# Linear attention into a top-1 mixture of experts: table rows by a one-hot, loads of the second expert behind gathers, paired narrow tiles, new plan keys

## The chip, the cores and the metric

One core of a Trainium2 chip. The metric is device time in microseconds of one execution. The kernel before takes 562.57 us, the median of 3 runs (562.14 to 563.09).

## The reference

Attention without softmax, a norm per head, and a mixture of experts with one expert per token, 4608 tokens of 512, 8 experts.

```
kv  = einsum('bhsd,bhse->bhde', k, v)          # 8 batches, 8 heads, 576 tokens, 64
out = einsum('bhsd,bhde->bhse', q, kv)
x   = out / sqrt(mean(out*out, -1) + 1e-6) * g_norm     # as rows of 4608 x 512
expert = argmax(x @ w_gate); gate = softmax(x @ w_gate)[expert]
# each expert takes its tokens in order, up to capacity
y = relu(x[tokens of e] @ w1[e]) @ w2[e]       # 512 x 1024 and 1024 x 512
out[token] = gate[token] * y
```

## The kernel before

Attention runs by batch. Tokens' heads are multiplied by the small kv matrix, squares are summed, logits and gates follow, and the unnormed rows with their factors go to x_dram in device memory. Each batch also enters its tokens in a table: for each expert, 6 columns of 128 slots (W = 48 columns), which token stands where. Tokens reach their experts by an indirect DMA (a gather) from x_dram with row numbers from that table.

The expert that has most tokens after three batches is fixed as the first (`pick`, line 1077). Its weights are loaded during attention, and after the fifth batch its first 384 slots are gathered and multiplied (`early_slots`, line 1168). The others are ranked by their number of tokens when attention is over (`rank_experts`, line 1090), and each rank has a fixed budget of slots (line 19: 704, 672, 640, 624, 592, 576, 560, 512). The first expert's slots 384 to 704 are done next, then the seven others.

At the seam, `finish` (line 1302) reads the table (`read_table`), cuts the first expert's 6 columns out of it at an address held in a register (`slots`, line 647), makes the target rows (`targets`) and ranks the experts. `rows` (line 1189) gathers the first expert's rest in three tiles; `rows_beside` (line 1618) gathers each later expert's in up to six, norms them, splits them into a high and a low half (`pair`) and turns them by a DMA transpose on SP's queue. `weights` (line 1567) loads w1 and w2 of each later expert on SP's queue in four parts each, takes the largest absolute value on VectorE (tile am), scales, and splits them into high and low float16. SP reads the expert's number from perm_i.

The products of an expert are (high + low) x (high + low) without the last term, three float16 products. The first one (`Gemm1`, into hp) leaves hh and hl, the high and low halves of the hidden rows. The second one (`Gemm2`, into yp) has the hidden rows as the stationary operand in tiles of 128 rows. A last tile of at most 112 rows is done turned round (`turned_products`, line 592): weights stationary, the few rows moving, 24 matmuls for each of 4 blocks of outputs; the result is copied (`keep`), turned back and scaled. Narrow tiles here: 64, 32, 112, 80, 64 and 48 rows for experts 1, 2, 4, 5, 6 and 7 in order.

The order on all engines is fixed before the run by a planner (`Plan`, line 105). It has engines as servers with estimated durations, takes at each step the operation that can start soonest, and among those that can start together the one with the lowest key. WAIT allows an engine operations that start a little later than the soonest. There are two plans, one for attention and one for the experts. The keys of single operations are moved by a list of numbers (NUDGE, line 74; by the number of the operation). The real waits are semaphores put in by the framework from the data; an engine runs its list in order.

## Time and profile before

| | us |
|---|---|
| median of 3 runs | 562.57 |
| the profiled execution | 560.41 |
| its span, first to last instruction | 558.5 |

| engine | busy us | share of the span |
|---|---|---|
| TensorE (PE) | 518.9 | 93% |
| VectorE (DVE) | 395.4 | 71% |
| ScalarE (ACT) | 253.8 | 45% |
| GpSimd (POOL) | 156.1 | 28% |

PE is TensorE's matmuls and PEld its weight loads. SP issues DMAs only. In the lists, L598 is line 598 of the kernel; a tile's name stands left of the arrow where it is written, right where it is read. A bracket behind an instruction tells how long its engine sat idle before it and what ended that; "issue" is a wait with no cause in the profile. Attention reaches to about 155 us, the first expert's rest to about 200, the other experts to the end.

### The profile page before, as it was taken

The numbers are of one execution on the slowest core, as the hardware profiler recorded it, in microseconds if no ns is written. First come the engines' busy times: TensorE is split into PE (matmuls) and PEld (weight loads), VectorE is DVE, ScalarE is ACT, GpSimd is POOL, SyncE is SP. The second block draws the span as 40 slices with busy tenths as digits, with TensorE's granted clock in tenths as the row PEclk, the third lists the DMA queues.
The fourth block names the chain that finished last, engine by engine and source line by source line (L and its number), as shares of the span: only waits on it lengthen the run. The fifth ranks groups of instructions, "written<-read, shape, count | busy, mean of one in ns | idle before, by whom it ended". The sixth has DMA issues, their size and how long they took to land.

```text
span 558.5 us, 12272 instructions
## 1 busy us (share of the span) xinstructions
PE 518.9 (93%) x4727; PEld 343.5 (61%) x4727; DVE 395.4 (71%) x1033; ACT 253.8 (45%) x508; POOL 156.1 (28%) x175
## 2 busy tenths in 40 slices
PE   2989979798977989999999999999999999999994
PEld 2878778675535566546764575577467648745442
DVE  3388868999938789899899896796968537721200
ACT  0577747786414373283553643452553525211210
POOL 6011010662347363132305402350234041012011
PEclk9999979799999999999999999999999999999998
DMA  8999999854195769589475760972688070011010
GB/s 270 352 350 323 358 391 364 262 189 187 43 343 147 213 195 302 136 242 264 124 258 134 231 223 19 221 232 101 164 145 253 3 123 34 1 39 39 0 40 31
DMA packets 78021, 102.61 MB, mean 184 GB/s; under 512 B 43222, under 2 KB 51414, under 8 KB 76932
## 3 DMA queue, kind: packets, MB, share of 16 engines
q1 hardware_dynamic: 69600, 70.43, 43.0%
q0 software_dynamic: 7776, 31.30, 16.3%
q8 instruction: 39, 0.64, 0.5%
q14 instruction: 26, 0.21, 0.1%
q10 hardware_dynamic: 580, 0.02, 0.1%
HBM read 73.13 MB, written 20.61 MB: 168 GB/s over the span
## 4 chain that ended last, share of the span: by engine, by line
PE 50%; DMA 18%; issue 18%; DVE 7%; ACT 3%; POOL 2%; SPq 0%; POOLq 0%; DVEq 0%; ACTq 0%
PE hp L543 17%; PE yp L589 15%; DMA out_dram<-ysb,si 9%; PE op L843 5%; DMA xs<-pair 4%; PE a L754 3%; PE qp L825 2%; PE op L543 2%; DMA q_sb<-in_q_dram 2%; DMA v_sb<-in_v_dram 1%; DMA xg<-x_dram,gi 1%; PE yp L598 1%; PE op L589 1%; DVE ss L876 1%; POOL pair L488 1%
## 5 line engine op out<-in xcount | busy, mean ns | idle before, releaser
L543 PE MATMUL hp<-xs,w1h 128*128 128x320 f16 (+6 forms) x896 | 133.4, 300 | 4.3 <-DMA xs<-pair 1.6
L543 PEld LDWEIGHTS <-w1h 128*128 128x128 f16 x960 | 93.2, 98 | 43.6 <-issue 5.6
L619 POOL DMA_INDIRECT out_dram<-ysb,si x41 | 47.1, 1150 | 246.1 <-ACT ysb L614 133.0
L589 PEld LDWEIGHTS <-hh 128*128 128x128 f16 x560 | 54.4, 98 | 62.8 <-issue 0.4
L548 ACT ACTIVATE hh<-hp 128x320 f16<-128x320 f32 (+7 forms) x64 | 40.8, 638 | 105.7 <-PE hp L543 105.4
L354 DVE TENSOR_REDUCE am<-raw 128x1 f32<-128x512 f32 x120 | 76.3, 675 | 2.6 <-DMA raw<-in_moe_w_dram 2.6
L543 PE MATMUL hp<-xs,w1l 128*128 128x320 f16 (+6 forms) x448 | 71.5, 300 | 0.0
L551 DVE SCALAR_TENSOR_TENSOR hl<-hp,hh 128x320 f16<-128x320 f32 (+7 forms) x64 | 47.3, 739 | 33.4 <-ACT hh L548 32.8
L589 PE MATMUL yp<-w2h,hh 128*128 128x512 f16 x272 | 65.0, 379 | 0.2 <-ACT ysb L614 0.2
L589 PE MATMUL yp<-w2h,hl 128*128 128x512 f16 x272 | 65.1, 379 | 0.0
L589 PE MATMUL yp<-w2l,hh 128*128 128x512 f16 x272 | 64.7, 379 | 0.0
L614 ACT ACTIVATE ysb<-yp,ysc 128x512 f32<-128x512 f32 (+5 forms) x40 | 27.3, 682 | 81.1 <-PE yp L589 67.7
L543 PEld LDWEIGHTS <-w1l 128*128 128x128 f16 x480 | 46.8, 98 | 19.2
L450 POOL DMA_INDIRECT xg<-x_dram,gi x41 | 44.1, 1075 | 28.9 <-DVE xm L458 11.3
L589 PEld LDWEIGHTS <-hl 128*128 128x128 f16 x280 | 27.1, 98 | 31.8
L394 DVE SCALAR_TENSOR_TENSOR w1l<-raw,sg,w1h 128x512 f16<-128x512 f32 x64 | 45.1, 741 | 1.7 <-ACT w1h L388 1.7
L843 PE MATMUL op<-kv_bd,qt 128*128 128x144 f32 x256 | 43.9, 309 | 1.8 <-ACT qt L695 0.7
L394 DVE SCALAR_TENSOR_TENSOR w2l<-raw,sw,w2h 128x512 f16<-128x512 f32 x64 | 44.4, 742 | 0.3 <-ACT w2h L388 0.2
L388 ACT ACTIVATE w2h<-raw,sw 128x512 f16<-128x512 f32 x62 | 39.7, 711 | 6.2 <-PE yp L598 3.6
L843 PEld LDWEIGHTS op<-kv_bd,qt 128*128 128x128 f32 x256 | 36.4, 202 | 4.7 <-ACT qt L695 1.2
L388 ACT ACTIVATE w1h<-raw,sg 128x512 f16<-128x512 f32 x60 | 38.6, 711 | 1.6 <-DVE sg L383 1.6
L484 ACT CAST pair<-xm 128x512 f16<-128x512 f32 (+5 forms) x35 | 21.4, 616 | 39.3 <-DMA xs<-pair 20.3
(245 smaller groups left out, 685.2 us busy)
## 6 DMA issues: line engine op xcount, KB each, us to landing
raw<-in_moe_w_dram SPq DMA_DIRECT2D x64, 512.0 KB, 5.4
k_sb<-in_k_dram SPq DMA_DIRECT2D x16, 576.0 KB, 7.4
v_sb<-in_v_dram SPq DMA_DIRECT2D x16, 576.0 KB, 7.2
x_dram<-o_sb POOLq DMA_DIRECT2D x8, 1152.0 KB, 8.5
q_sb<-in_q_dram SPq DMA_DIRECT2D x16, 512.0 KB, 7.6
x_dram<-o_sb POOLq DMA_DIRECT2D x8, 144.0 KB, 8.5
q_sb<-in_q_dram SPq DMA_DIRECT2D x32, 32.0 KB, 6.8
xg<-x_dram,gi POOLq DMA_INDIRECT x41, 4.8
```

What stands on the lines that cost most here:

```text
L354: nc.vector.tensor_reduce(out=am()[:, p:p + 1], in_=raw[:, sl(p)], axis=AX.X, op=ALU.max, apply_absolute_value=True)
L388: nc.scalar.activation(wh[:, sl(p)], raw[:, sl(p)], AF.Copy, scale=z["s"])
L394: nc.vector.scalar_tensor_tensor(out=wl[:, sl(p)], in0=raw[:, sl(p)], scalar=z["s"], in1=wh[:, sl(p)], op0=ALU.mult, op1=ALU.subtract)
L450: nc.gpsimd.indirect_dma_start(out=self.xg[i][0:n], out_offset=None, in_=x_dram[0:self.rows, :], in_offset=bass.IndirectOffsetOnAxis(ap=se ...
L484: nc.scalar.copy(self.pair[i][0:n, 0], self.xm[i][0:n])
L543: nc.tensor.matmul(self.view(hp)[:, u], lhsT=w[:, c, j * P:(j + 1) * P], rhs=x[:, c, u * hw:(u + 1) * hw], start=(t == 0 and c == 0), stop ...
L548: nc.scalar.activation(self.out(self.hh, j), self.view(hp), AF.Relu)
L551: nc.vector.scalar_tensor_tensor(out=self.out(self.hl, j), in0=self.view(hp), scalar=0.0, in1=self.out(self.hh, j), op0=ALU.max, op1=ALU.s ...
L589: nc.tensor.matmul(yp[0:n, 0:DM], lhsT=h[:, j, o:o + n], rhs=w[:, j, :], start=(m == 0), stop=(m == len(self.terms) - 1))
L614: nc.scalar.activation(self.ysb[0:n], yp[0:n, 0:DM], AF.Copy, scale=self.ysc[0:n, i:i + 1])
L619: nc.gpsimd.indirect_dma_start(out=out[:, :], out_offset=bass.IndirectOffsetOnAxis(ap=self.sidx[0:n, col:col + 1], axis=0), in_=ysb[0:n], ...
L843: nc.tensor.matmul(y, lhsT=qt.t[:, i * P:(i + 1) * P], rhs=kv2[:, half * HH + i], start=True, stop=True)
```

## The change

The first expert's 6 columns are no longer copied at a register's address. They are picked by a product with the one-hot of the first expert, a sum and a max, both in the early cut and in `finish`. The table of all experts' sources (`gidx_tab`) is made in a step of its own, and only in `finish`. The rank is split in four steps, with a later key. WAIT lets GpSimd's plan take operations that start up to 0.15 later, in both plans. The second expert's w1 loads read its number from a new cell, which GpSimd copies from perm_i after the first expert's three gathers. Turned tiles of at most 64 rows take hh and hl in one matmul with the high weights, as an operand in two pieces (hh and hl now lie in one tile); the two halves of the result are added in `keep`. The list of moved keys of attention's plan is new throughout; the experts' plan still has none. Durations that the planner assumes are changed with it.

```diff
-WAIT = {}
+WAIT = {"P": 0.15}
...
+TURNED_PAIR = {64: 2.7, 48: 2.2, 32: 1.8}
-NUDGE = {
-    5: 1, 22: 1.1, 30: -9, 50: 7.6, 67: 3.4, 97: 5.8, 152: 5.6, 157: 6.2, 161: 12.3, 175: 1.1, 179: 4.5, 221:
...
+NUDGE = (
+    {79: 1.6, 93: 2.6, 148: 0.4, 162: -1, 176: 1.8, 184: -8.3, 187: -5.1, 188: 10.3, 220: 0.3, 229: -4, 267:
...
+    {})
...
         def hidden(self):
-            self.hh, self.hl = (self.pool.tile([P, KF, self.size], F16, name=x, bufs=1) for x in ("hh", "hl"))
+            self.hb = self.pool.tile([P, 2, KF, self.size], F16, name="hb", bufs=1)
+            self.hh, self.hl = self.hb[:, 0], self.hb[:, 1]
...
         def turned_products(self, i, yp):
-            terms = self.terms[0:KF] + self.terms[2 * KF:] + self.terms[KF:2 * KF]
+            both = n <= PAIRED
+            m = 2 * n if both else n
             for dt in range(KD):
-                for m, (h, w, j) in enumerate(terms):
-                    nc.tensor.matmul(yp[:, dt * n:(dt + 1) * n], lhsT=w[:, j, dt * P:(dt + 1) * P],
-                                     rhs=h[:, j, o:o + n], start=(m == 0), stop=(m == len(terms) - 1))
+                ds_ = slice(dt * P, (dt + 1) * P)
+                y = yp[:, dt * m:(dt + 1) * m]
+                terms = [(self.w[0], self.g.hb[:, :, j, o:o + n], y.rearrange("p (u x) -> p u x", u=2), j) for j in range(KF)] if both else \
+                    [(w, h[:, j, o:o + n], y, j) for h, w, j in self.terms[0:KF] + self.terms[2 * KF:]]
+                terms += [(w, h[:, j, o:o + n], y[:, 0:n], j) for h, w, j in self.terms[KF:2 * KF]]
+                for k_, (w, x, y_, j) in enumerate(terms):
+                    nc.tensor.matmul(y_, lhsT=w[:, j, ds_], rhs=x, start=(k_ == 0), stop=(k_ == len(terms) - 1),
+                                     skip_group_check=both)
...
+            if n <= PAIRED:
+                nc.vector.tensor_reduce(out=self.yt[:, 0:KD * n].rearrange("p (c x) -> p c x", c=KD),
+                                        in_=yp[:, 0:2 * KD * n].rearrange("p (c u x) -> p c x u", c=KD, u=2), axis=AX.X, op=ALU.add)
+            else:
+                nc.vector.tensor_copy(self.yt[:, 0:KD * n], yp[:, 0:KD * n])
...
-    plan = Plan(FREE, NUDGE)
+    plan = Plan(FREE, NUDGE[0])
...
+        return (0.62, compare), (0.5, rank), (0.5, turn), (0.28, keep)
...
+    def sources_of_first(gi):
+        s3 = [P, NHI, E]
+        mine = sm.tile(s3, F32, name="mine", bufs=1)
+        nc.vector.tensor_tensor(out=mine, in0=early["tab"].rearrange("p (e h) -> p h e", e=E),
+                                in1=first.rearrange("p (o e) -> p o e", o=1).broadcast_to(s3), op=ALU.mult)
+        g = sm.tile([P, NHI], F32, name="mine_g", bufs=1)
+        nc.vector.tensor_reduce(out=g, in_=mine, axis=AX.X, op=ALU.add)
+        nc.vector.tensor_scalar(out=gi, in0=g, scalar1=0.0, scalar2=None, op0=ALU.max)
...
     def early_slots():
         def cut(e):
+            early["gi"] = ep.tile([P, NHI], I32, name="gi_first")
+            sources_of_first(early["gi"])
+
+        def cut2(e):
             early["first"] = {"c": nc.vector.value_load(first_i[0:1, 1:2], min_val=0, max_val=(E - 1) * NHI)}
-            early["gi"], = slots(ep, early["first"], ("gi",))
...
     def finish():
-        o = op(("V", 0.75), lambda e: read_table(), enters[-1:] + early["slots"] + early["slots2"], key)
+        t = op(("V", 0.45), lambda e: read_table(), enters[-1:] + early["slots"] + early["slots2"], key)
         def cut(e):
-            early["gi0"], = slots(ep, early["first"], ("gi",), EARLY)
+            early["gi0"] = ep.tile([P, NHI], I32, name="gi_rest")
+            sources_of_first(early["gi0"])
...
-        early["cut"] = o = op(("V", 0.2), cut, [o], key)
-        o2 = op(("V", 0.6), cut2, [o], key + 0.2)
+        early["cut"] = op(("V", 0.65), cut, [t], key)
+        early["sources"] = op(("V", 0.2), lambda e: sources(), [t], key + 0.1)
+        early["cut2"] = op(("V", 0.8), cut2, [t], key + 0.3)
         o = count(cnt_all, key)
-        early["rank"] = op(("V", 2.5), lambda e: rank_experts(cnt_all), [o], key + 0.1)
-        early["cut2"] = o2
+        for long, f in rank_steps(cnt_all):
+            o = op(("V", long), lambda e, f=f: f(), [o], key + 0.2)
+        early["rank"] = o
...
-                    regs["e"] = nc.sync.value_load(perm_i[0:1, 0, r:r + 1], min_val=0, max_val=E - 1)
+                    which = next_i if r == 1 and i == 0 else perm_i[0:1, 0, r:r + 1]
+                    regs["e"] = nc.sync.value_load(which, min_val=0, max_val=E - 1)
...
-            before = [] if r > 1 else sent
+            before = []
+            if r == 0:
+                before = [op(("P", 0.12), lambda e: nc.gpsimd.tensor_copy(next_i, perm_i[0:1, 0, 1:2]),
+                             [early["rank"]] + sent, -KEY / 2)]
+            elif r == 1:
+                before = sent
```

## Rows read from the trace of the kernel before

**Rows 1.** Busy time by stage: PE, PEld, DVE, ACT, POOL; clock, DMA share, GB/s.

```profile
20.00:100.00 80.00, 73.04 (x1300) 64.26 (x1298) 61.34 (x207) 55.85 (x154) 9.37 (x12) 0.96 1.04 360
...
124.00:136.00 12.00, 9.77 (x72) 7.07 (x71) 12.00 (x34) 9.67 (x29) 4.16 (x4) 1.00 0.51 205
...
163.30:171.60 8.30, 3.28 (x21) 2.15 (x22) 4.40 (x10) 2.64 (x5) 3.82 (x4) 1.00 0.63 224
171.60:186.30 14.70, 13.51 (x97) 9.41 (x97) 13.17 (x33) 4.09 (x9) 9.72 (x12) 1.00 0.72 218
186.30:203.10 16.80, 14.61 (x154) 8.20 (x153) 12.95 (x31) 9.54 (x16) 9.26 (x8) 1.00 0.49 122
203.10:540.00 336.90, 336.41 (x2439) 206.34 (x2440) 240.40 (x525) 138.87 (x221) 81.97 (x90) 1.00 0.51 143
```

**Rows 2.** Timeline of GpSimd: start, us, instruction [idle before <- what ended it].

```profile
152.87 0.57 POOL L1051 DMA_DIRECT2D x_dram<-o_sb  x1
...
158.57 1.03 POOL L450 DMA_INDIRECT xg<-x_dram,gi  x1 [2.84 <-DVE gi L655]
159.90 0.95 POOL L450 DMA_INDIRECT xg<-x_dram,gi  x1 [0.31 <-DMA out_dram<-ysb,si]
161.16 0.94 POOL L450 DMA_INDIRECT xg<-x_dram,gi  x1 [0.30 <-issue]
...
163.72 0.93 POOL L450 DMA_INDIRECT xg<-x_dram,gi  x1 [0.30 <-issue]
...
166.90 0.96 POOL L450 DMA_INDIRECT xg<-x_dram,gi  x1 [2.25 <-DVE gt L465]
```

**Rows 3.** Times to landing: last x_dram write; gathers 158-164, 166-178; weight loads 156-159.

```profile
DMA to landing us min/median/max: 4.6/4.6/4.6
...
DMA to landing us min/median/max: 5.1/6.9/7.3
...
DMA to landing us min/median/max: 3.5/4.2/4.8
...
DMA to landing us min/median/max: 5.7/6.0/6.3
```

**Rows 4.** Timeline of VectorE, same columns as rows 2.

```profile
154.67 0.20 DVE L1107 TENSOR_SCALAR perm_i<-perm 128x8 int32<-128x8 f32 x1
...
156.60 0.17 DVE L655 COPY gi<-gidx_tab 128x6 int32 x1 [1.15 <-issue]
...
167.96 0.69 DVE L458 TENSOR_TENSOR xm<-xg 128x512 f32<-128x512 f32 x1 [1.33 <-DMA xg<-x_dram,gi]
...
181.18 0.68 DVE L354 TENSOR_REDUCE am<-raw 128x1 f32<-128x512 f32 x1
```

**Rows 5.** Chain that ended last, 140 to 205: start, us, what.

```profile
161.16 6.78 DMA xg<-x_dram,gi
...
182.19 6.79 DMA xs<-pair
...
199.99 2.98 DMA xs<-pair
...
203.10 2.01 PE hp L543 x13
```

**Rows 6.** Timeline of the SP queue, same columns as rows 2.

```profile
156.28 2.31 SPq L338 DMA_DIRECT2D raw<-in_moe_w_dram  x4
```

**Rows 7.** Timeline of TensorE, same columns as rows 2.

```profile
171.54 1.90 PE L543 MATMUL hp<-xs,w1h 128*128 128x320 f16 x12 [1.06 <-ACT xs L695]
```

**Rows 8.** Line 598 alone: PE, PEld busy; tiles of 64, 32, 80 rows.

```profile
196.00:201.00 5.00, 2.96 (x96) 2.94 (x96) 1.00 0.28 54
256.00:260.00 4.00, 2.55 (x96) 2.55 (x96) 1.00 1.06 322
411.00:415.50 4.50, 3.60 (x96) 3.56 (x96) 1.00 0.57 117
```

**Rows 9.** Instructions on tile yt: duration in ns min/median/max, first and last start.

```profile
L604 DVE COPY yt<-yp x6: 292/425/616, 200.0 to 509.7; 128x256 f32<-128x256 f32 x2, 128x128 f32<-128x128 f32 x1, 128x448 f32<-128x448 f32 x1, 128x320 f32<-128x320 f32 x1
```

More of the change, by code (lines that the diff above doesn't have):

```diff
@@ L27 @@
 NARROW = 112
+PAIRED = 64
 XS = 8.0
@@ L1088, in pick, with rank_steps @@
         nc.vector.tensor_copy(first_i, fe)
-    def rank_experts(cnt):
-        d = distinct(cnt)
-        nc.vector.scalar_tensor_tensor(out=d, in0=first, scalar=BIG, in1=d, op0=ALU.mult, op1=ALU.add)
+    def rank_steps(cnt):
+        z = {}
         sq3 = [P, E, E]
@@ L1623, in cut @@
             st["gi"], st["si"] = slots(mo, perm_i[0:1, 1, r:r + 1], ("gi", "si"))
-        cut_ = op(("V", 0.4), cut, [early["rank"], early["cut2"]], key, (sl,))
+        cut_ = op(("V", 0.62), cut, [early["rank"], early["sources"], early["cut2"]], key, (sl,))
         n = len(spans(0, BUDGET[r]))
```

48 lines of the change are left out of this document (27 added, 21 removed), and 10 rows, old and new, of the table NUDGE.

## The prediction

> **What bounds the kernel now.** I read the busy time by stage first, then the chain that ended last around the seam between attention and the experts, then the instruction lists of TensorE, GpSimd, VectorE and the SP queue in that seam, then the times to landing. By stage [rows 1]: up to 100 us the DMA engines are full (1.04), and TensorE is idle for 7.0 of 80 us without being the limit. From 124 to 136 VectorE is full, 12.00 of 12.00. From 203.1 to 540 TensorE is busy for 336.4 of 336.9 us: there a microsecond of matmuls is a microsecond of the end, and an earlier start of this stretch is an earlier end. Between them lies the seam, where TensorE is idle for 5.0 (163.3 to 171.6), 1.2 (to 186.3) and 2.2 us (to 203.1), 8.4 us in all. Most that this change can win is there.
>
> The seam goes like this. The last write of x_dram starts at 152.87 [rows 2] and lands after 4.6 us, at 157.5 [rows 3]. The first expert's gather indices are ready at 156.77 (156.60 + 0.17) [rows 4], so before the landing, and the first gather starts at 158.57 [rows 2]. Four gathers start at 158.57, 159.90, 161.16 and 163.72. VectorE's norm of the first expert's second tile, at 167.96, waits for the gather of 161.16 [rows 4, 5]; so the one of 159.90 is already the second expert's, and the first expert's third and last one is that of 163.72. SP has sent the second expert's four w1 loads, a quarter of 512 x 1024 float32 each, from 156.28 on, ahead of all of them [rows 6]. These gathers take 5.1 to 7.3 us (median 6.9); the five sent after 166.8, when w1 has landed, take 3.5 to 4.8 (median 4.2) [rows 3]. The third gather lands at 163.72 + 5.1 = 168.8, and the first expert's remaining products start at 171.54 [rows 7]. The stretch ends with TensorE waiting, at 203.10, for the last DMA transpose of the second expert's rows, sent at 199.99 [rows 5].
>
> **The one-hot and the later rank.** Removed from the path to the first expert's indices: a copy at a register's address, which starts 1.15 us after the instruction before it [rows 4], and the rank, nine small VectorE instructions in front of the table, the last at 154.67, some 2 us in all. Added: a product, a sum and a max over 48 numbers per row, about 0.2 us each, as the small step of 154.67; the copy took 0.17. The indices come 1 to 2 us earlier, at about 155, but the gather cannot start before the landing at 157.5. I cost this at nothing; what hides it is the x_dram write. If the new keys bring that write forward, up to 158.57 - 156.77 = 1.8 us of it shows; that stays in the range. The same three instructions in the fifth batch's early cut lie shortly ahead of the stretch where VectorE is full: three at 0.2, less the copy (0.17) and the table step that is left out there (0.2): +0.2 us, taken as on the path. Later users of the rank (the second expert's row slots, its w2 loads) have it by about 157, since nothing else fills VectorE before the gathers land.
>
> **The order of the gathers.** With a wait of 0.15 allowed for GpSimd the planner takes the first expert's second and third gather, which become ready 0.1 after the first, before the second expert's first one. The third moves from the fourth place to the third, 163.72 to about 161.17, for nothing; the second expert's first gather moves back by about 3 us, and had time: it landed at about 159.90 + 6.9 = 166.8, while its norm stands in VectorE's queue behind that of 167.96 and the third tile's.
>
> **The loads behind the gathers.** SP now reads the second expert's number from a cell that GpSimd copies after the third gather, so the four w1 loads really wait for it. What is queued on SP behind them (transposes of the second expert's rows, w2) started only after 176 anyway; the copy itself is one element on GpSimd, ahead of the next gather, and below half of a gather's issue (0.95). The copy is done at about 162.4. From the rank's write, 154.87, to the first load, 156.28, SP took 1.4 us [rows 4, 6]; so the loads go out from 163.8 to 166.1 and land 5.7 to 6.3 later [rows 3], at 169.5 to 172.1. Their users are the eight maxima on VectorE, whose last ran at 181.18 to 181.86 [rows 4]; moved forward by 4 us that is 177.9, so 5.8 us remain for eight of 0.68 = 5.4. It fits, barely.
>
> The first expert's gathers are then alone. With 4.2 us the third lands at 161.17 + 4.2 = 165.4 instead of 168.8, 3.4 earlier; what followed took 2.7 us (168.8 to 171.54), part of it a queue behind the second tile, which now goes ahead in time. Bounds for the start of the products: 3.4 earlier (same 2.7) and 5.0 (TensorE's 3.28 us of work there without any idle [rows 1]); I take 4.0. For the end of the seam the second expert's transposes must move as far. They start from the same gathers and free buffers (the gather of 166.90 waits for the first tile's gate copy [rows 2]), so they move too, but the w1 loads are now in flight over the first of them; a transpose beside loads took 6.79 us, a quiet one 2.98 [rows 5]. I take 0.4 for that, so 3.6 us are won at 203.1, with bounds 1.0 (one slow transpose more, about 3 us lost) and 5.0.
>
> **Paired narrow tiles.** Tiles of 64, 32, 64 and 48 rows (experts 1, 2, 6 and 7 in order) go from 96 matmuls to 64: 32 of twice the width, 32 of the old width. Busy times of 96 [rows 8]: 64 columns 2.96 us, 30.8 ns each; 80 columns 3.60, 37.5; 32 columns 2.55, 26.6. From 64 to 80 columns each costs 0.42 ns; below 64 stands a floor, at which I put 48 too. A pair of 64 is 128 columns, 30.8 + 64 x 0.42 = 57.7; of 48, 96 columns, 44.2; of 32, 64 columns, 30.8. Per tile: 64 rows 32 x (57.7 + 30.8) = 2.83 against 2.96; 48 rows 32 x (44.2 + 26.6) = 2.27 against 2.55; 32 rows 32 x (30.8 + 26.6) = 1.84 against 2.55. Won: 0.13, 0.28 and 0.71, and 0.13 for the first expert's, which ends in the wait before 203.10 and is not counted. Sum 1.1; the end of the last matmul is spread over 96 in these quotients, so 1.0. VectorE's copy (0.29 to 0.62 [rows 9]) becomes a sum over twice as much, about 0.25 more; it's hidden, because after 203.1 TensorE works on the next expert between product and turn. Bounds: 1.1, and a loss, below.
>
> **New keys in attention.** The same work in another order. Until 100 us DMA is the limit, from 124 to 136 VectorE. I take 0. For both sides I take TensorE's idle time where VectorE is full, 2.2 of 12 us [rows 1].
>
> **Sum.** -3.6 - 1.0 + 0.2 + 0 = -4.4 us. The profiled execution took 560.41 (span 558.5 and 1.9 around it), so 556.0; the median of the runs, 562.57, is 2.2 above that one, and gives 558.2.
>
> **Rivals.**
> 1. The loads come late for VectorE. Its maxima may stand in its queue from 167.5 on, when the products start, while the first part lands at 169.5 to 170.1; it stands for up to 2.6 us with the low halves of the first expert's hidden rows behind it, and TensorE behind these. For it: the sum above has 0.4 us to spare. Against: TensorE has two banks of products as cover. -4.4 + 2.6 gives 560.8. Chance 0.17.
> 2. Slower: the copy isn't right behind the third gather but behind one that waits for a buffer, as that of 166.90 does. Then it ends at about 167.9, the first load goes out at 169.3 and lands at 175.0, VectorE stands for 7.5 us: -4.4 + 7.5 gives 565.7. It decides from a copy at about 165 on: there the wait eats all 4.4 us. Against: the copy's key lies between those of the two experts, and 0.15 is allowed. Chance 0.08.
> 3. The change doesn't do what it says: the gathers are slow by themselves, three at once with a write, and stay at 6.9. The third lands at 161.17 + 6.9 = 168.1, 0.7 earlier: -0.7 - 1.0 + 0.2 gives 561.1. Against: the gather of 163.72, last beside the loads, already took 5.1. Chance 0.06.
> 4. The keys cost 2.2 us or more where VectorE is full: 560.4 to 563. Chance 0.07.
> 5. A pair's weight load is not hidden in front of an operand in two pieces: one floor of 26 ns more on each of 32 pairs, 0.8 us per tile, 2.5 over the three that count: 558.2 + 2.5 = 560.7. Against: in the rows above 64 columns the step is the columns' alone. Chance 0.05.
> The Trainium skill, "TensorE: Matmul & The Clock Gate", section "Back-to-back issue gap", gives about 81 ns as the sustained spacing of matmuls of 128 columns with their weight loads. By that a pair of 64 would be dearer than two single ones here, and pairing would be no gain. The rows at 64 and 80 columns lie on that section's shorter formula instead, so I give the 81 little weight; no row of this kernel has 128 columns of this type.
>
> **How the numbers follow.** The forecast has 0.57. Its own range is 555 to 560.5. The low end is 5.0 + 1.1 + 2.2 below 562.57, so 554.3; the high end reaches over rivals 1, 3, 5 and most of 4, to 562.6. Left out are rival 2 and the ends of the others. A measurement of this kernel can tell about 0.2%, 1.1 us: faster is below 561.4. From the forecast 0.55, from rival 1 0.11, from the rest 0.09: 0.75 faster. Same 0.14, half of it from rivals 1 and 4. Slower 0.11, mostly rival 2.
>
> **What would show it.** Right: three gathers of the first expert one after another, landing after about 4 us; w1 loads after 163; products from about 167.5; the next expert's first full product at about 199.5; narrow tiles at 2.8, 1.8 and 2.2 us. Wrong: gathers still near 7 us, VectorE idle before a maximum and a product waiting for a low half, a transpose chain that ends at 202, a pair spaced at 80 ns, or TensorE idle for over 15 us from 20 to 136.

## The result, and the profile after

The changed kernel took 569.3 us (median, 565.2 to 571.4) against 562.4 for the kernel before in the same set: ratio 1.0112, 95% interval 1.0079 to 1.0146. The forecast was 558.2 with a range to 562.6; the kernel became slower, by 7 us where 4 less were expected. The same kernel in two more sets, each on another chip: 563.9 against 561.2 (1.0021, 0.9985 to 1.0057) and 568.9 against 563.5 (1.0110, 1.0058 to 1.0163). So the loss of 1.1% stands in two of three sets, and on the third chip the kernel is level with the one before; in no set is there the gain that was forecast.

The profiled execution took 565.2 (span 563.4, against 558.5). I split both spans at the first product of each of the first three experts in the order of computing; the view gives TensorE's busy time first in each stretch, then the weight loads', VectorE's, ScalarE's and GpSimd's, the granted clock, DMA share and GB/s. Kernel before:

```profile
136.00:171.54 35.54, 30.21 (x187) 16.47 (x183) 25.08 (x101) 11.44 (x24) 15.20 (x15) 1.00 0.52 187
171.54:201.20 29.66, 27.86 (x249) 17.55 (x248) 24.42 (x56) 12.44 (x23) 17.67 (x18) 1.00 0.60 166
201.20:259.26 58.06, 56.47 (x413) 33.14 (x413) 52.88 (x103) 29.64 (x47) 19.80 (x24) 1.00 0.83 250
259.26:364.47 105.21, 105.21 (x719) 64.36 (x715) 90.22 (x191) 49.09 (x78) 27.59 (x32) 1.00 0.63 176
364.47:551.44 186.97, 186.48 (x1372) 113.95 (x1369) 99.06 (x238) 62.71 (x100) 37.83 (x38) 1.00 0.33 87
```

Changed kernel, the same stretches:

```profile
136.00:170.69 34.69, 32.34 (x190) 17.48 (x188) 26.84 (x101) 11.74 (x27) 16.37 (x17) 1.00 0.46 161
170.69:201.41 30.72, 29.08 (x216) 18.26 (x216) 24.75 (x57) 13.47 (x25) 14.80 (x18) 0.94 0.75 204
201.41:263.19 61.78, 57.95 (x382) 33.22 (x380) 54.67 (x106) 30.29 (x48) 20.99 (x23) 0.94 0.83 237
263.19:370.21 107.02, 105.59 (x719) 64.41 (x716) 89.97 (x190) 48.10 (x76) 25.95 (x33) 1.00 0.59 173
370.21:556.70 186.49, 185.84 (x1308) 113.63 (x1305) 97.50 (x233) 63.26 (x100) 36.81 (x37) 1.00 0.28 85
```

Up to the first product 0.85 us are won, where 4.0 were expected; the first expert's stage is 1.06 longer, the second's 3.72, the third's and fourth's 1.81, the rest 0.48 shorter: 5.26 at TensorE's end. In the second expert's stage idle time grew from 1.59 to 3.83 us and busy time from 56.47 to 57.95, at a mean clock of 0.94. In the first expert's stage busy time grew as well, from 27.86 to 29.08: the granted clock was 0.52 from 172.3 to 175.6.

The gathers came as forecast. GpSimd in the changed kernel (start, us, instruction, idle before):

```profile
150.53 0.56 POOL L1066 DMA_DIRECT2D x_dram<-o_sb  x1
...
158.63 1.03 POOL L454 DMA_INDIRECT xg<-x_dram,gi_rest  x1 [0.86 <-issue]
159.96 0.97 POOL L454 DMA_INDIRECT xg<-x_dram,gi_rest  x1 [0.30 <-issue]
161.23 0.93 POOL L454 DMA_INDIRECT xg<-x_dram,gi_rest  x1 [0.30 <-issue]
162.16 0.18 POOL L1759 COPY next_i<-perm_i 1x1 int32<-1x1 int32 x1
```

Three gathers one after another, the copy right behind them, and VectorE's three norms at 162.21, 163.85 and 164.65, where before they ran at 165.87, 167.96 [rows 4] and 169.23. From there the gain is lost at four places, besides the stretch at half clock in the first expert's stage. First, ScalarE's copy of the third tile, whose transposes TensorE had issued from 166.91 to 167.37:

```profile
165.89 0.59 ACT L710 CAST xs<-xp 128x512 f16<-128x512 f32 x1 [0.91 <-PE xp L474]
170.27 0.37 ACT L710 CAST xs<-xp 128x256 f16<-128x256 f32 x1 [3.79 <-PE yp L594]
```

It came 2.9 us behind their end, and the products at 170.69 behind it. Second, VectorE stood for 2.55 us (1.73 + 0.82) at the maxima of the second expert's weights, with the low half of the first expert's third tile (171.63) and the second expert's first norm (171.96) behind them:

```profile
168.93 1.28 DVE L358 TENSOR_REDUCE am<-raw 128x1 f32<-128x512 f32 x2 [1.73 <-DMA raw<-in_moe_w_dram]
171.03 0.69 DVE L358 TENSOR_REDUCE am<-raw 128x1 f32<-128x512 f32 x1 [0.82 <-DMA raw<-in_moe_w_dram]
171.63 0.41 DVE L482 TENSOR_TENSOR xs<-xp,xs 128x256 f16<-128x256 f32 x1
171.96 0.68 DVE L462 TENSOR_TENSOR xm<-xg 128x512 f32<-128x512 f32 x1
```

Before, that norm stood directly behind the first expert's last one; now it is 7.3 us behind. The kernel before:

```profile
169.23 0.67 DVE L458 TENSOR_TENSOR xm<-xg 64x512 f32<-64x512 f32 x1
169.89 0.67 DVE L458 TENSOR_TENSOR xm<-xg 128x512 f32<-128x512 f32 x1
```

Third, TensorE waits for the last transpose of the second expert's rows, 1.59 us before and 3.83 now, and resumes at half clock. TensorE before, then changed:

```profile
203.10 2.30 PE L543 MATMUL hp<-xs,w1h 128*128 128x336 f16 x15 [1.59 <-DMA xs<-pair]
```

```profile
205.54 4.36 PE L548 MATMUL hp<-xs,w1h 128*128 128x336 f16 x15 [3.83 <-DMA xs<-pair]
```

The same fifteen matmuls took 4.36 us instead of 2.30; the granted clock was 0.50 from 205.54 to 209.97, so the level of 1.2 GHz; it had fallen at about 203.4, during the wait. Fourth, in the third expert's stage VectorE stood at a copy of the row slots of an expert to come:

```profile
273.70 0.17 DVE L670 COPY si<-sidx_tab 128x6 int32 x1 [2.96 <-DMA out_dram<-ysb,si]
```

The slot lists have four buffers, and this one is released when the second expert's last scatter, issued at 271.5, has landed 2.2 us later. Low halves of hidden rows wait behind the copy. In the kernel before that scatter went out at 265.1, and the copy waited for nothing:

```profile
270.16 0.17 DVE L655 COPY si<-sidx_tab 128x6 int32 x1
```

### The profile page after: what moved, and what is told of

The parts are those of the page before. It is cut to its first block, busy times and chain, and to the rows that moved or that the text cites. A ratio compares the mean times of both kernels' runs of the same rounds, so it can differ in the third digit from the quotient of the medians.

```text
span 563.4 us, 12034 instructions
## 1 busy us (share of the span) xinstructions
PE 523.4 (93%) x4599; PEld 344.9 (61%) x4599; DVE 395.1 (70%) x1042; ACT 254.8 (45%) x506; POOL 147.4 (26%) x172
## 4 chain that ended last, share of the span: by engine, by line
PE 49%; issue 20%; DMA 13%; DVE 10%; ACT 3%; POOL 3%; SPq 0%; POOLq 0%; another core or an unknown queue 0%; DVEq 0%; ACTq 0%
PE yp L594 17%; PE hp L548 15%; DMA out_dram<-ysb,si 8%; PE op L858 4%; PE op L548 2%; DMA raw<-in_moe_w_dram 2%; PE qp L840 2%; PE a L769 2%; PE yp L609 2%; DMA v_sb<-in_v_dram 1%; POOL xg L454 1%; DVE ss L891 1%; DVE w2l L398 1%; PE op L861 1%; DVE hb L556 1%
## 5 line engine op out<-in xcount | busy, mean ns | idle before, releaser
L548 PE MATMUL hp<-xs,w1h 128*128 128x320 f16 (+6 forms) x896 | 137.0, 304 | 8.1 <-DMA xs<-pair 3.8
L594 PEld LDWEIGHTS <-hb 128*128 128x128 f16 x840 | 81.3, 98 | 95.0 <-issue 0.4
L594 PE MATMUL yp<-w2h,hb 128*128 128x512 f16 x544 | 125.5, 379 | 0.2 <-ACT ysb L629 0.2
L634 POOL DMA_INDIRECT out_dram<-ysb,si x41 | 49.6, 1210 | 261.5 <-ACT ysb L629 210.9
L553 ACT ACTIVATE hb<-hp 128x320 f16<-128x320 f32 (+7 forms) x64 | 40.9, 638 | 117.0 <-PE hp L548 112.3
L556 DVE SCALAR_TENSOR_TENSOR hb<-hp,hb 128x320 f16<-128x320 f32 (+7 forms) x64 | 47.3, 739 | 40.3 <-ACT hb L553 39.0
L594 PE MATMUL yp<-w2l,hb 128*128 128x512 f16 x272 | 64.6, 379 | 0.0
L454 POOL DMA_INDIRECT xg<-x_dram,gi x35 | 37.8, 1080 | 27.4 <-issue 12.8
L488 ACT CAST pair<-xm 128x512 f16<-128x512 f32 (+5 forms) x35 | 21.5, 614 | 26.7 <-DVE xm L462 12.2
L769 PE MATMUL a<-v_sb,k_sb 64*64 64x64 f32 x576 | 23.7, 233 | 9.7 <-DMA v_sb<-in_v_dram 7.7
L769 PEld LDWEIGHTS a<-v_sb,k_sb 64*64 64x64 f32 x576 | 20.7, 145 | 12.1 <-issue 11.0
```

The costliest lines, as they stand in the source:

```text
L454: nc.gpsimd.indirect_dma_start(out=self.xg[i][0:n], out_offset=None, in_=x_dram[0:self.rows, :], in_offset=bass.IndirectOffsetOnAxis(ap=se ...
L548: nc.tensor.matmul(self.view(hp)[:, u], lhsT=w[:, c, j * P:(j + 1) * P], rhs=x[:, c, u * hw:(u + 1) * hw], start=(t == 0 and c == 0), stop ...
L553: nc.scalar.activation(self.out(self.hh, j), self.view(hp), AF.Relu)
L556: nc.vector.scalar_tensor_tensor(out=self.out(self.hl, j), in0=self.view(hp), scalar=0.0, in1=self.out(self.hh, j), op0=ALU.max, op1=ALU.s ...
L594: nc.tensor.matmul(yp[0:n, 0:DM], lhsT=h[:, j, o:o + n], rhs=w[:, j, :], start=(m == 0), stop=(m == len(self.terms) - 1))
L634: nc.gpsimd.indirect_dma_start(out=out[:, :], out_offset=bass.IndirectOffsetOnAxis(ap=self.sidx[0:n, col:col + 1], axis=0), in_=ysb[0:n], ...
```

## The experiments

One table first; "gather" is the first expert's first rest gather, "product" its first rest product, "late" the start of the third tile's copy behind its transposes, in the profiled execution. The time of the kernel before is that of the same set; rows with the same time of it are of one set, and each set ran on a chip of its own. The change itself is in three of the sets, so other runs can be set beside it only by their ratios.

| run | us | before | ratio, 95% interval | gather | product | distance | late |
|---|---|---|---|---|---|---|---|
| before (profiled) | | | | 158.57 | 171.54 | 12.97 | 0.65 |
| the change | 569.3 | 562.4 | 1.0112 (1.0079 to 1.0146) | 158.63 | 170.69 | 12.06 | 2.89 |
| loads_free | 572.1 | 562.7 | 1.0144 (1.0075 to 1.0213) | 159.88 | 176.59 | 16.71 | 0.04 |
| old_keys | 561.6 | 562.7 | 0.9970 (0.9943 to 0.9998) | 159.28 | 171.42 | 12.14 | 3.61 |
| paired_only | 561.7 | 562.7 | 1.0007 (0.9975 to 1.0039) | 157.46 | 170.89 | 13.43 | 0.78 |
| tops_late | 562.6 | 562.7 | 0.9999 (0.9971 to 1.0027) | 160.01 | 172.22 | 12.21 | 3.16 |
| loads_later | 560.4 | 561.0 | 0.9996 (0.9967 to 1.0026) | 155.30 | 165.62 | 10.32 | 0.04 |
| keys_tops | 561.3 | 561.0 | 1.0017 (0.9985 to 1.0049) | 160.36 | 170.12 | 9.76 | 0.04 |
| free_old | 561.9 | 561.0 | 1.0011 (0.9978 to 1.0044) | 160.01 | 173.88 | 13.87 | 0.04 |
| wait_p | 563.9 | 561.0 | 1.0061 (1.0027 to 1.0094) | 158.16 | 172.67 | 14.51 | 0.09 |
| after_again | 563.9 | 561.2 | 1.0021 (0.9985 to 1.0057) | 157.33 | 167.83 | 10.50 | 0.04 |
| new_keys | 565.2 | 561.2 | 1.0074 (1.0047 to 1.0101) | 157.97 | 175.63 | 17.66 | 0.04 |
| later_tops | 558.6 | 561.2 | 0.9956 (0.9934 to 0.9978) | 155.22 | 165.56 | 10.34 | 0.04 |
| later_old | 563.6 | 561.2 | 1.0034 (1.0005 to 1.0063) | 157.53 | 167.29 | 9.76 | 0.81 |
| after_third | 568.9 | 563.5 | 1.0110 (1.0058 to 1.0163) | 157.79 | 169.99 | 12.20 | 2.98 |
| slots8 | 565.3 | 563.5 | 1.0033 (1.0005 to 1.0061) | 158.67 | 170.89 | 12.22 | 3.00 |
| best8 | 563.9 | 563.5 | 1.0002 (0.9972 to 1.0031) | 161.14 | 171.55 | 10.41 | 0.04 |
| tops8 | 557.6 | 561.5 | 0.9924 (0.9896 to 0.9953) | 155.71 | 166.04 | 10.33 | 0.04 |
| later_tops2 | 559.1 | 561.5 | 0.9968 (0.9947 to 0.9989) | 156.30 | 166.74 | 10.44 | 0.04 |
| tops8_2 | 555.6 | 561.1 | 0.9902 (0.9885 to 0.9918) | 156.51 | 166.91 | 10.40 | 0.04 |

**One part undone, or one part alone.** Theory A: the loads behind the gathers make VectorE's maxima late. B: the new keys cost. C: the pairing costs. `loads_free` takes the loads' wait back:

```diff
-                    which = next_i if r == 1 and i == 0 else perm_i[0:1, 0, r:r + 1]
-                    regs["e"] = nc.sync.value_load(which, min_val=0, max_val=E - 1)
+                    regs["e"] = nc.sync.value_load(perm_i[0:1, 0, r:r + 1], min_val=0, max_val=E - 1)
```

> The changed kernel with the second expert's loads put back: they wait for the rank alone, not for a copy on GpSimd behind the first expert's gathers. All else as in the changed kernel. Theory A (the loads come too late for VectorE, whose maxima stand in its queue ahead of the second expert's first norm): the first norm of the second expert comes before 170.5 instead of 171.96, the last transpose lands before 203 instead of 205.5, the wait of 3.8 us and the stretch at half clock behind it go, and the time falls by 3 to 5 us, to 0.2 to 0.4% above the kernel before. Theory B (the new keys cost it): within 1 us of the changed kernel. Theory C (pairing, with both halves of the hidden rows in one tile, costs it): within 1 us of the changed kernel.

It was no faster, 572.1. VectorE's norms of the first expert show why (start, us, idle before):

```profile
167.16 0.69 DVE L462 TENSOR_TENSOR xm<-xg 128x512 f32<-128x512 f32 x1 [3.99 <-DMA xg<-x_dram,gi_rest]
169.25 0.69 DVE L462 TENSOR_TENSOR xm<-xg 128x512 f32<-128x512 f32 x1 [1.33 <-DMA xg<-x_dram,gi_rest]
170.72 0.68 DVE L462 TENSOR_TENSOR xm<-xg 64x512 f32<-64x512 f32 x1
```

The loads start at 158.91, 1 us ahead of the gathers, and the norms start 7.3 and 8.0 us after the first two gathers, where the change has 3.6 and 3.9. TensorE stood for 3.2 us before the first transposes, ran at half clock from 167.6 to 174.4, and the first product is at 176.59; the wait for the last transpose was 3.62 us all the same. So the loads' wait is worth its place, and theory A can't be that it is bad by itself.

`old_keys` is the change with attention's old keys (`NUDGE` as before, the second plan without keys).

> The changed kernel with the keys of attention's plan from the kernel before. Theory B (new keys): the time falls by 5 us or more, to that of the kernel before or below, with the last table entry at about 153.5 instead of 155.5. Theory A (late loads): the table entry may move by 2 us, but maxima still stand before the second expert's first norm and TensorE still waits over 3 us for the last transpose; the time falls by 2 us at most. Theory C: within 1 us of the changed kernel.

561.6, level or 0.3% below: this looked like theory B. `paired_only` is the kernel before with `hidden`, `turned_products` and `keep` of the change; the times in the plan are those of the kernel before.

> The kernel before with the pairing of narrow tiles alone (both halves in one tile, the sum on VectorE). Theory C (pairing costs): slower than the kernel before by 2 us or more, with new waits of ScalarE or VectorE around the hidden rows. Theories A and B: faster by 0.7 to 1.1 us (tiles of 64, 48 and 32 rows at 2.8, 2.2 and 1.8 us).

Level; theory C, a loss of 2 us or more, is all but out (the interval ends at 2.2 us). But the gain of 0.7 to 1.1 us isn't seen in the time either; its profile has a stretch at half clock that the kernel before has not (last section). `tops_late` moves the maxima 3.5 us back in the order worked out for VectorE, nothing else:

```diff
-                                   (raws[p // 2],)))
+                                   (raws[p // 2],), late=3.5 if r == 1 and i == 0 else 0.0))
```

> The changed kernel with the planner told that the eight maxima of the second expert's w1 can start 3.5 us later, so that they stand behind the second expert's first norm in VectorE's list; nothing else is edited, the plan of the experts follows from it. Theory A: the first norm of the second expert comes by 169 instead of 171.96, the last transpose lands by 203, TensorE's wait before it falls from 3.8 to under 2 us, and the time falls by 3 to 6 us, to that of the kernel before or below. Theories B and C: within 1 us of the changed kernel.

562.6, level with the kernel before (0.9999), where the change was at 1.0112 in its set and the copy was late as well. TensorE waits 0.03 us for the last transpose instead of 3.83, although the first product is no earlier (172.22). Not all of that is won. Just ahead, TensorE now waits for the maximum that the weights are scaled by (tile bmax), 1.82 us where it was 0.93 (the view gives us in total, times, longest):

```profile
PE yp L624 <- DVE bmax L382: 1.8, 1, 1.8
```

So the two waits there take 1.85 us together, in the change 4.76, in the kernel before 2.20 (0.61 + 1.59). And the first norm did not come by 169, as expected, but at 172.54, no earlier than in the change: with the maxima moved it stood behind the low half of the first expert's third tile, and this behind the late copy:

```profile
172.20 0.42 DVE L482 TENSOR_TENSOR xs<-xp,xs 128x256 f16<-128x256 f32 x1 [3.50 <-ACT xs L710]
172.54 0.68 DVE L462 TENSOR_TENSOR xm<-xg 128x512 f32<-128x512 f32 x1
```

The edit shows that the place of the maxima in VectorE's list makes the wait. That they make it by holding up the first norm is seen only where the copy is on time: from the first gather to that norm it is 12.48 us in `after_again`, and 9.48 and 9.52 in `tops8` and `tops8_2` (below), which have this edit.

**Is it the loads, or the keys?** `loads_later` puts the copy that releases the loads behind the second expert's third gather:

```diff
-                             [early["rank"]] + sent, -KEY / 2)]
+                             [early["rank"]] + own + asked[:3], -KEY / 2)]
```

(`rows_beside` is called first; `own` is the first expert's `sent`.)

> The changed kernel, with the copy that releases the second expert's loads put behind that expert's first three gathers instead of ahead of the first, so that the six loads of 512 KB start about 5 us later (169 instead of 163.6 us). In the profile of the changed kernel the copy of the first expert's third tile waited until 170.27 though its transposes had been issued by 167.15, while the loads filled the DMA engines. Theory C1 (the loads in flight hold up TensorE's signal and SyncE's own instructions): the third copy follows its transposes within 0.5 us, and the first expert's products start at about 167.7 to 168.7 instead of 170.69. Theory C2 (the delay belongs to the order of the work on TensorE, not to the loads): the products start at 170 to 172 as before. For the time: VectorE's maxima come later still if they stand where they stood (rival 1 of the prediction), so with C1 alone at about 566 to 571, and 2 to 3 us less than the changed kernel only if the wait for the last transposes at 205.5 doesn't grow with it.

The third copy came on time and the distance from gather to product was 10.32, but TensorE then waited 3.0 us near 169 and 3.1 near 199: 560.4, level with the kernel before. `keys_tops` has the old keys and the later maxima:

> The changed kernel with both of the edits that each took its loss away: attention's keys of the kernel before, and the second expert's maxima 3.5 us later in the order worked out for VectorE. If the two losses are separate (keys 7.7 us, place of the maxima 6.7 us in the first comparison), the time falls to about 555 to 557. If they are one loss that either edit avoids (a lineup of late gathers, maxima ahead of the second expert's first norm, and a half-clock stretch behind the wait for the last transposes), it comes out with them, at 560.5 to 562.5.

They do not add up: 561.3. `free_old` is old keys without the loads' wait:

> The changed kernel with the old keys and without the loads' wait (the load's register read from the rank, as before), so that beside the run with old keys alone it shows what the loads' place behind the gathers is worth under the old keys. By the prediction's step (c): the first expert's gathers land 2 to 3.4 us later than with the wait, the products start 2.5 to 5 us later than 171.4, and the time is 1.0 to 5.0 us above 561.6. By the theory that the order of the gathers already gives the gain and the loads' wait only moves the wait to VectorE's maxima: within 1 us of 561.6.

The loads' place is worth 4.1 us at the product (13.87 against 9.76 of `keys_tops`, which has the later maxima too; the copy is on time in both), and 0.1% or nothing in time. `wait_p` is the kernel before with `WAIT = {"P": 0.15}`:

> The kernel before with GpSimd's tolerance of 0.15 us in the order's choice alone: the first expert's three gathers come next to each other, nothing else. By the prediction: the third gather is issued 2.5 us sooner, but the products still wait for data behind the weight loads, so 562.0 to 562.7, no difference. It is also the look at whether signals of TensorE come late (over 0.5 us behind the last recorded matmul) in a kernel that is nearly the one before, on the chip of these runs: in the profile of the kernel before none does. If the lateness comes with the change, there is none here either; if it comes with the chip of the day, there are some.

Not level but 0.6% slower. The third norm ran at 168.90, a little sooner than before (169.23); but TensorE, idle for 3.45 us ahead of the first transposes, was at half clock from 165.1 to 171.9, and the product came at 172.67.

**The change again, and keys alone.**

> The changed kernel itself once more, on another chip or at another time. In its first profile TensorE's signals came up to 2.9 us behind the recorded ends of its matmuls between 163 and 170, SyncE's single instructions took up to 0.7 us there, and the first expert's products started at 170.69; in a second set of runs (loads later, both edits, old keys without the wait, the tolerance alone) no signal was late by over 0.25 us. Theory D (the loss was mostly that lateness, and goes with the chip or the execution): no late signals here, first products at 166 to 168, and a time within 0.4% of the kernel before, 561 to 563. Theory A (the loss is built into the order: maxima ahead of the second expert's first norm, the last transposes late, TensorE at half clock behind that wait): no late signals, first products at 166 to 168, and still a wait for the last transposes of 3 us or more near 203 and a time 1% above the kernel before, 566 to 569.

The profiled execution is the longest of the ten, 568.1 us. In it the third copy came on time:

```profile
164.08 0.58 ACT L710 CAST xs<-xp 128x512 f16<-128x512 f32 x1 [0.79 <-PE xp L474]
166.20 0.37 ACT L710 CAST xs<-xp 128x256 f16<-128x256 f32 x1 [1.53 <-PE xp L474]
```

The product is at 167.83, 3.7 us earlier than before. Yet TensorE resumes for the second expert at 203.53 behind a wait of 3.71 (3.68 in `after_third`, below), and stands for 4.06 near 272 (3.18). So theory D (only the late copy) falls as the whole cause. The time, 563.9 with runs from 558.9 to 568.1, lies between what the two theories gave and cannot be told from the kernel before; that the late copy is part of the loss in the other two sets fits this, and was not tested by itself.

`new_keys` is the kernel before with the change's keys:

> The kernel before with the new keys of attention's order and nothing else of the change: the one part that was only run together with the others. By the prediction: no difference, 0 with bounds of 2.2 us, 560 to 565. By theory B (the new keys cost by themselves, what the run with old keys seemed to show): 6 to 8 us slower, 567 to 570, with the last table entry about 2 us later than 153.5 and the first gather later than 158.6.

0.7% slower, with the first gather no later (157.97). In its profile TensorE ran at half clock from 156.1 to 162.9, took the first tile's transposes at 170.81, behind the products that it was late with, though the norm had ended at 164.86, and later waited 3.9 us for the last transpose of the second expert's rows. Theory B in the form "attention takes longer" is not seen: over all profiles the first gather starts at 157.5 to 160.4 with the old keys and at 155.2 to 161.1 with the new. That the keys cost at the seam is seen here and not in `loads_later` and `tops8`, which have them too.

`later_tops` is `loads_later` with the maxima of `tops_late`, `later_old` is `loads_later` with the old keys:

> The changed kernel with the second expert's loads behind that expert's third gather and its maxima 3.5 us later in VectorE's order. Each alone came out level with the kernel before. With the loads later the first products started at 165.62, 5.9 us earlier than before, and TensorE then waited 3.0 us at 169 behind VectorE and 3.1 us at 199 for the last transposes. If the wait at 199 comes from VectorE's maxima standing ahead of the second expert's norms, it shrinks to under 1.5 us here and the time is 556 to 559. If it comes from GpSimd's order (the last pair behind scatters that wait for TensorE's own products) or from ScalarE, it stays near 3 us, and the time is 560 to 562.

> The changed kernel with the loads behind the third gather and with the old keys, against the run with old keys alone (loads ahead of the second expert's gathers, 561.56). If the loads in flight are what holds up the first products under either set of keys, the products start 3 to 5 us sooner than 171.4 and the time falls to 558 to 560. If what TensorE gains there it waits for at the second expert's transposes, the time stays at 560.5 to 562.5, with an idle stretch of 3 us or more near 200.

The first is 0.4% faster than the kernel before, the second 0.3% slower.

The time of `later_tops` came out as its first branch has it, the wait as the second: TensorE still waits 2.85 us for the last transposes (2.92 in `later_tops2`, 2.76 in `best8`, and 3.02 in `keys_tops`, which also has the later maxima). Here the second expert's first three norms start at 163.03, 166.51 and 168.52, ahead of every maximum, and the chain to the last transpose goes through GpSimd, whose last `pair`, at 192.31, stands behind a scatter issued at 191.29. So the maxima are one cause of that wait and GpSimd's order is another; no run moved the latter alone. In `later_old` the product came 4.1 us sooner than in `old_keys`, as expected, but TensorE waited 3.73 us near 174 for a low half of the hidden rows and 3.13 for the last transposes, and 563.6 lies above both forecasts.

**The wait for the slot lists.** `slots8` is the change with more buffers; the order of instructions on every engine is the same. `after_third` is the change unaltered, beside it.

```diff
-            t = pool.tile([P, NHI + 1], I32, name=f"{nm}{s0}", bufs=4)
+            t = pool.tile([P, NHI + 1], I32, name=f"{nm}{s0}", bufs=8)
```

> The changed kernel a third time, as the measure for the next run on the same chip: 561 to 569 by the two sets so far (569.3 and 563.9), with VectorE idle 3 to 5 us near 272 ahead of the copy of the fourth next expert's slots.

> The changed kernel with eight buffers for the experts' slot lists in place of four; the order of every engine's instructions is the same. Theory E (VectorE stands at the copy of the slots until the second expert's last scatter has landed, 2.96 us in the first profile of the changed kernel, 4.60 in the second and 5.02 with the loads free; TensorE runs dry behind it for 0.9 to 4.1 us and in two of the three runs at half clock for 3.4 us after): the idle stretch near 272 is gone on VectorE and on TensorE, and the time is 2 to 5 us below the changed kernel of the same set. Rival: TensorE only reaches another wait sooner (weights or rows of the third expert, its banks), and the time is within 1 us of the changed kernel's.

VectorE in `after_third`, then in `slots8`:

```profile
267.87 0.39 DVE L670 COPY gi<-gidx_tab 128x6 int32 x1
272.98 0.17 DVE L670 COPY si<-sidx_tab 128x6 int32 x1 [4.72 <-issue]
```

```profile
270.21 0.15 DVE L670 COPY gi<-gidx_tab 128x6 int32 x1
270.28 0.15 DVE L670 COPY si<-sidx_tab 128x6 int32 x1
```

The stretch of the third and fourth expert, the same two kernels:

```profile
260.22:371.38 111.16, 107.26 (x719) 65.11 (x715) 90.50 (x190) 48.87 (x78) 26.00 (x33) 0.98 0.58 167
```

```profile
261.57:366.78 105.21, 105.21 (x719) 64.31 (x715) 90.28 (x190) 49.15 (x78) 28.06 (x33) 1.00 0.61 180
```

5.95 us less here, 3.6 in the median (568.9 to 565.3). Theory E holds: the wait near 272 is the buffer's. The wait for the last transpose is untouched by it (3.69). With `best8`, the order of `later_tops` and eight buffers:

> The fastest order so far (second expert's loads behind its third gather, its maxima 3.5 us later) with the eight buffers. There VectorE stood 4.45 us at that copy, at 310 to 315, but TensorE had only 0.61 us idle in that expert and 0.06 in the next. Theory E with cover (the wait costs only where TensorE runs dry behind it): 0 to 1 us below 558.6, so 557.5 to 558.8. If the copy's wait costs its whole length: 554 to 555.

Level in a set where the change was 1.1% slower; no run set it beside `later_tops`, so what the buffers gave there is open.

**Both waits taken away.** `tops8` is `tops_late` and `slots8` together; `later_tops2` is `later_tops` once more.

> The changed kernel with the second expert's maxima 3.5 us later in VectorE's order and eight buffers for the slot lists: the two waits taken away one at a time so far (TensorE waited 0.03 us for the second expert's last transposes with the first edit; the second took 3.6 us off). If both waits were given-back gain, this is the version in which the 3.6 us of step (c) come through: 2 to 5 us below the kernel before on this chip. If TensorE finds the next wait (rows of the third expert, its own late signals), it is level with the kernel before, within 1.5 us.

> The order that came out 0.44% below the kernel before (558.6 against 561.2) once more, here on the chip of the run beside it. If that gain is the order's, 0.3 to 0.6% below the kernel before again; if it is only there where TensorE's signals are not late (with eight buffers the same order was level, 1.0002, on a chip where the third tile's signal came 3.0 us late), level here when the profile shows such signals, faster when it doesn't.

0.76% and 0.32% faster than the kernel before. In `tops8` the wait for the last transpose is 0.48 us, that for bmax ahead of it 1.83. `tops8_2` is the same kernel as `tops8`:

> The version with both waits taken away (maxima 3.5 us later, eight buffers) once more. In the runs so far the third tile's copy came 2.9 to 3.6 us behind its transposes in five of eight profiles with the second expert's loads 3.7 to 5.8 us behind the first gather, and 0.04 us behind in the other three, each chip showing one of the two. If the copy is on time here too, the distance from first gather to first product is 10.3 to 10.5 us and the time 0.5 to 1.0% below the kernel before; if it is late, the distance is 12.1 to 12.2 us and the time 0.1 to 0.5% below it.

555.6 against 561.1. Its stretches, cut as above:

```profile
136.00:166.91 30.91, 30.06 (x176) 16.22 (x175) 24.60 (x93) 9.84 (x20) 15.00 (x15) 1.00 0.44 151
166.91:197.55 30.64, 27.86 (x217) 17.60 (x216) 23.17 (x56) 13.65 (x25) 16.51 (x20) 1.00 0.73 223
197.55:254.91 57.36, 57.18 (x381) 32.77 (x380) 53.69 (x102) 29.67 (x47) 20.00 (x21) 0.97 0.88 239
254.91:361.33 106.42, 105.70 (x719) 64.30 (x716) 90.16 (x191) 48.79 (x78) 29.94 (x34) 1.00 0.63 182
361.33:547.00 185.67, 185.67 (x1308) 113.72 (x1305) 99.02 (x237) 62.84 (x100) 36.90 (x37) 1.00 0.27 85
```

Against the kernel before: -4.63 at the first product, +0.98, -0.70, +1.21, -1.30, together -4.44. Of the 4.63 at the first product, 2.06 are an earlier first gather (156.51 against 158.57), 2.57 a shorter distance from it. This version beats the kernel before in both sets, and the change by its ratio; the change itself was not run on these two chips, and this version not on a chip where the third copy comes late.

## Why the prediction was wrong, step by step

- **One-hot and later rank, 0.** Right in what it says: the first gather starts at 158.63 against 158.57 [rows 2]. The x_dram write went out 2.3 us earlier (150.53 against 152.87), and still the gather was not earlier in this profile; in others of the same keys it was, by up to 3.3 us, and in one, `best8`, 2.6 later.
- **Order of the gathers, for nothing.** Right about the order and the third gather's time, wrong about the price where it stands alone: `wait_p` was 0.6% slower, with a half-clock stretch in its profile that no step priced.
- **Loads behind the gathers, first half.** The gathers took 3.6 and 3.9 us to their norms, where 4.2 was forecast for the landing. From gather to product it was 10.5 us where the third copy came on time, 2.5 less than before and 3.2 less with the old keys (9.76), against 4.0 forecast and bounds of 3.4 to 5.0: a little too much. In the profiled execution of the change it was 0.9, because of the late copy, which no rival named.
- **Loads behind the gathers, second half: this is the step that failed.** "For the end of the seam the second expert's transposes must move as far", and, since they start from the same gathers and free buffers, "so they move too". They didn't. TensorE resumed behind the last transpose at 205.54 instead of 203.10, and even with the product at 167.83 only at 203.53. The transposes start from VectorE's norms, and the maxima stood ahead of the first of these in VectorE's list, waiting for their loads; with the maxima moved and the buffers added TensorE resumes at 197.54 and 198.22 (`tops8`, `tops8_2`; their first gathers are 2.9 and 2.1 us earlier than before). GpSimd's order can hold the transposes up too (`later_tops`). That is rival 1, with the right queue and in part the wrong neighbour: VectorE stood for 2.55 us, as priced (up to 2.6), but behind it stood the low half of the first expert's third tile and the second expert's norm, not only the low halves of the first expert's hidden rows. The prediction's own "It fits, barely" was the warning.
- **What no step priced.** The half clock at 205.54: 2.1 us on fifteen matmuls. Over the profiles it goes with the paired tiles, not with the longer wait alone (last section). The same list of slots that had waited for nothing before: 5.95 us of the third and fourth expert's stretch in `after_third`. The seam was treated as a place where a microsecond late costs a microsecond; here 2.44 us late at 205.54 became 5.26 at the end.
- **Rival 2** did not occur: the copy stood right behind the third gather. **Rival 3** neither: the gathers were not slow by themselves.
- **Paired tiles, -1.0.** Right for the matmuls themselves, not seen in the time. Busy time of the paired line in `slots8`, tiles of 64, 32 and 48 rows:

```profile
196.00:201.00 5.00, 2.88 (x64) 2.86 (x64) 1.00 0.37 107
256.00:262.00 6.00, 1.89 (x64) 1.88 (x64) 1.00 1.15 278
...
505.00:513.00 8.00, 2.32 (x64) 2.31 (x64) 1.00 0.16 66
```

  2.88, 1.89 and 2.32 us, forecast 2.83, 1.84 and 2.27; before 2.96, 2.55 [rows 8] and 2.56. Less 32 x 30.8 ns for the single ones, a pair of 64 takes 59 ns, so rival 5 is out. The Trainium skill, "TensorE: Matmul & The Clock Gate", section "Back-to-back issue gap", gives 81 ns for matmuls of 128 columns with their weight loads; this trace does not agree. In the time of `paired_only` 1 us is within its interval; in its profile the half clock behind the first expert's paired tile takes 1.57 us on fifteen matmuls, more than the pairs save. The prediction left that tile out of its sum as ending in a wait.
- **New keys, 0 within 2.2.** Right about attention's length, wrong that nothing else depends on them: `new_keys` cost 4 us, nearly twice the bound. In its profile (568.5 us) it is at the seam: the first product is 4.1 us later, the wait for the last transpose 2.3 longer, and TensorE resumes at half clock. So rival 4 had the size of the cost and not the place, which it put where VectorE is full. Which key does it was not tried.

With both waits removed the profile stands 4.44 us below the one before, where the prediction's sum was 4.4. That is luck in good part: 2.06 us of it are the earlier first gather, which the prediction put at nothing; the distance from gather to product gave 2.57 where 4.0 were forecast, and 0.98 was lost in the first expert's stage.

## What to carry to other kernels

An earlier start is won only when each queue behind it is followed to the next engine: list, for the moved transfer, which engine's instruction waits for it and what stands behind that instruction, for whichever work it belongs. When TensorE's wait grows, price the clock after it as well as the wait. When a wait is gone, add up the idle time of the whole stretch: in `tops_late` 0.9 us of it had only moved to the wait ahead. A ring of buffers that is just free in time is part of an order: look for copies that wait for a buffer when the work ahead of them slips by a few us, and try one more buffer before another order.

## What the runs showed of the hardware

- **A late third copy.** Where the second expert's loads start 4.5 to 5.1 us behind the first gather, the third tile's copy came 2.9 to 3.6 us behind the recorded end of its transposes in five profiles and 0.04 us behind in the four others; every chip of these runs showed one of the two. On a chip where it was late (`after_third`, `slots8`), the kernel whose loads start at 172.8 (`best8`) had it on time. That fits a delay that needs both the loads in flight and the chip, and does not show it: there is one profiled execution for each kernel and chip. In the change the SP queue's own instructions stretch as well: a register move that takes 29 ns in `after_again` and in the kernel before took up to 701 ns. The two do not always go together: `best8` had a move of 600 ns and the copy on time, `old_keys` and `tops_late` no move over 29 ns and the copy late. What causes either stays open. Where the copy was late, the distance from gather to product was 1.7 us longer (12.2 against 10.5).

```profile
L342 SPq MOVE raw<-in_moe_w_dram x6: 3/16/701, 163.6 to 169.5; - x6
```

```profile
L342 SPq MOVE raw<-in_moe_w_dram x6: 29/29/29, 162.4 to 166.6; - x6
```

  The first row is the change, the second `after_again`: instruction, duration in ns min/median/max, first and last start.
- **Half clock after short waits.** In the kernel before TensorE runs at half clock only in attention and after its last matmul. In all other profiles here except one (`wait_p`) it also stood at half for 3 to 7 us between 197 and 214. Some had short waits there: `tops_late` idled 1.82 us before 201.66 and was at half clock from 201.8 to 205.2. The 17 profiles with paired tiles all have it; of the three without, only `new_keys` does, behind a wait of 3.90 us. `paired_only`, which differs from the kernel before by the pairing alone, waited 0.88 + 1.40 us there, the kernel before 0.61 + 1.59 without it:

```profile
203.01 3.87 PE L545 MATMUL hp<-xs,w1h 128*128 128x336 f16 x15 [1.40 <-DMA xs<-pair]
```

  The same fifteen matmuls take 2.30 us in the kernel before. Over whole executions the mean granted clock was 0.982 in ten runs of `paired_only` and 0.986 in 25 of the kernel before in the same set. So the half clock seems to come with the paired tile that ends just ahead of the wait; with one profile of each kernel that is not shown.
